# Attention and two feed-forward blocks on one core: instruction order from a list scheduler instead of an order written by hand

## Chip, cores and metric

One Trainium2 chip, 1 core. The metric is the device time of one execution in microseconds (us). The kernel before took 1174.35 us, the median of 3 runs (1172.29 to 1177.39).

## The reference

Three steps over N = 6016 rows, C = 256, all in float32, the weights stored as float64:

```
s    = (k/|k|).T @ (q/|q|) / tau         # 256 x 256, norms over N
a    = softmax(s)                        # over the last axis
x    = v @ a                             # 6016 x 256
xn   = x / sqrt(mean(x*x) + 1e-6) * rms_g
y    = (silu(xn @ w_gate) * (xn @ w_val)) @ w_out       # 256 -> 1536 (twice) -> 256
h    = y @ w_in2
out  = (h - tanh(h)) @ w_out2                           # 256 -> 2048 -> 256
```

## The kernel before

Everything is computed transposed: 128 channels on the partitions, up to 512 rows of N on the free axis. A float32 product is split in a high and a low part of type fp32r (`hi_of` on ScalarE, L138, writes the high part; `lo_of` on VectorE, L144, the rest), and `prod` (L146) issues three matmuls for it: wh·xh, wl·xh, wh·xl. So each operand of TensorE costs one ScalarE and one VectorE instruction. Some small products use full float32 matmuls, which the profile records as two matmuls each.

The work runs in five parts.

1. **Scores** (`attention`, L396): 47 tiles of q and k arrive in 13 chunks; 94 float32 products add up in two PSUM banks, ScalarE squares q and k, VectorE adds the squares. Of the last `BEHIND` = 3 chunks the products for the first bank are issued first, then the norms (`nrm`), then the products for the second bank. `WARM` = 8 float32 products on ones come ahead of the first data.
2. **Softmax, x and its norm** for blocks 0 and 1 (512 and 384 rows): `x_full`, `x_post`.
3. **Gate blocks** (`gate_block`, L1007): block pair 0 with plain products, 12 slices `f` of the hidden width; block 1 runs `SKEW` = 2 slices behind. Beside it the float64 weights are turned to float32 in nine `items` (L255: gv0, gv1, w10, gv2, gv3, w11, gv4, gv5, w12), each of two ScalarE and four VectorE instructions on 128x1024 (`conversion`, L289), and the x of pair 1 (blocks 2 and 3) is made.
4. **Five block pairs of the first feed-forward** with 7 instead of 8 block products (`unit`, L815, twice in each of 6 units, `first_unit`, L863). Each pair also makes the x and the operands of the next pair (`x_operands`, L660, `operands`, L621). The row norm takes a path over DRAM: TensorE sums the squares (`ms`), the row goes out (`row`), comes back narrow (`nar`), VectorE takes the root, it goes out again (`back`) and is broadcast to 128 partitions (`rs`, L765), and VectorE multiplies four x tiles by it (L771). Beside it the weights of the second feed-forward are converted (`second_weights`) and sums of weight blocks are formed (`first_sums`, `second_sums`).
5. **Six block pairs of the second feed-forward** (`second_unit`, L1195), 8 units each.

Products with an output weight (`acc`) are not issued where their operand is made; they wait in a list, `fillers`, and `fill(n)` issues some at fixed places of a `unit`, to occupy TensorE while another engine works on a bank.

The order on each engine is written by hand: main steps as in the code, side work as generators (`Work`) whose next VectorE or ScalarE step is let in by `side(a, d)` at fixed places with fixed counts (`SIDE`, `SIDES`, `EARLY`, `PLAN`). A generator that needs a transfer waits for a number of such places (`yield 4` behind the issue of `rs`). Each engine runs its own queue in order, SyncE (SP) the DMAs' queue.

Of the kernel before, what the change touches and what calls it, by code (L numbers as in the profile page):

```python
# [1 line left out]

# [11 lines left out]
AX = mybir.AxisListType  # L14
# [10 lines left out]
LAST_CHUNKS = [2, 1]  # L25
BEHIND = 3
WARM = 8

EARLY = (((0, 1), (0, 0), (0, 0)), ((0, 1), (0, 0), (0, 0)), ((1, 1), (0, 1), (0, 0)))
SIDES = (((1, 2), (1, 2), (1, 1)), ((1, 2), (1, 2), (1, 1)))  # L30
RSQRT_SEED = float(0x5F3759DF)

REBIAS = 2.0 ** -112


class Work:
# [3 lines left out]


    clock = 0

    def __init__(self, steps):
        self.steps, self.kind, self.ready, self.done = steps, None, None, False

        self.last = dict(A=-1, D=-1, pe=-1)
        self.advance()

    def advance(self):  # L50
        got = next(self.steps, self)
        self.kind = self.ready = None
        if got is self:
            self.done = True
        elif callable(got):
            self.ready = got
        elif isinstance(got, int):
            at = Work.clock + got
            self.ready = lambda: Work.clock >= at
        else:  # L60
            self.kind = got

    def can(self, kind):
        while self.ready and self.ready():
            self.advance()
        return self.kind == kind and self.last[kind] < Work.clock

    def run(self):
        if self.kind in self.last:
            self.last["A" if self.kind == "D" else "D"] = Work.clock  # L70
        self.advance()
# [3 lines left out]
def attn_moe_kernel(  # L75
# [14 lines left out]

# [29 lines left out]
    dram = ctx.enter_context(tc.tile_pool(name="dram", bufs=1, space=bass.MemoryType.DRAM))  # L120

    def bank(tag, name):
        return ps.tile([P, BLK], F32, tag=tag, name=name)
# [5 lines left out]
    def psum(name):  # L129

        turn[0] += 1
        return bank(WORK[(turn[0] - 1) % 4], name)

    def f32(t):
        return t.bitcast(F32)

    def hi_of(dst, src, scale=1.0):
        nc.scalar.activation(out=dst, in_=src, func=AF.Copy, scale=scale)  # L138

    def copy(dst, src):  # L140
        nc.scalar.activation(out=dst, in_=src, func=AF.Copy)  # L141

    def lo_of(dst, src, hi):
        nc.vector.tensor_sub(out=dst, in0=src, in1=f32(hi))  # L144

    def prod(out, w, x, start):  # L146

        (wh, wl), (xh, xl) = w, x
        for i, (a, b) in enumerate(((wh, xh), (wl, xh), (wh, xl))):
            nc.tensor.matmul(  # L150
                out, a, b, start=start and i == 0, stop=i == 2, skip_group_check=True)

    def rsqrt_ops(m, y, t):

        ops = [lambda: nc.vector.tensor_scalar(
            out=y.bitcast(I32), in0=m.bitcast(I32), scalar1=-0.5, scalar2=RSQRT_SEED,
            op0=ALU.mult, op1=ALU.add)]
        for _ in range(3):
            ops += [
                lambda: nc.vector.scalar_tensor_tensor(  # L160
                    out=t, in0=y, scalar=-0.5, in1=m, op0=ALU.mult, op1=ALU.mult),
                lambda: nc.vector.tensor_mul(out=t, in0=t, in1=y),
                lambda: nc.vector.scalar_tensor_tensor(
                    out=y, in0=t, scalar=1.5, in1=y, op0=ALU.add, op1=ALU.mult),
            ]
        return ops

    def add(o, a, b):
        nc.vector.tensor_add(out=o, in0=a, in1=b)  # L169


    works = []

    def side(a=0, d=0):

        Work.clock += 1
        for kind, count in (("D", d), ("A", a)):
            for _ in range(count):
                w = next((w for w in works if w.can(kind)), None)
                if w:  # L180
                    w.run()
        works[:] = [w for w in works if not w.done]


    urgent = []

    def hurry():
        while urgent:
            urgent.pop(0)()

    def between():

        w = next((w for w in works if w.can("pe")), None)
        if w:
            w.run()

    def force(w, until):
        while not until():
            assert not w.done
            w.run()  # L200
            hurry()
# [4 lines left out]
    def narrow_tile(x, b):  # L206
        return wpool.tile([P, NARROW], F32, tag=f"nar{x}", name=f"nar{x}{b}")


    for x in "myt":  # L210
        narrow_tile(x, "")
    tau_t = wpool.tile([P, 1], F32, tag="tau", name="tau_t")
    g_t = wpool.tile([P, KC], F32, tag="g", name="g_t")
# [7 lines left out]
    make_identity(nc, ident)  # L221

    def act_tile(tag, bufs, name, dt=F32R, shape=None):
        return act.tile(shape or [P, BLK], dt, tag=tag, bufs=bufs, name=name)

    def buffer(tag, bufs, dt=F32R):
        return lambda name: act_tile(tag, bufs, name, dt)

    ox, oh, ol = buffer("ox", 5, F32), buffer("oh", 10), buffer("ol", 10)
    ut, uh, ul = buffer("ut", 4, F32), buffer("uh", 4), buffer("ul", 4)
    cs, sq_tile, sq_part = buffer("cs", 3, F32), buffer("sq", 4, F32), buffer("sq", 4)

    V2 = [P, KC, BLK]

# [19 lines left out]
    for i in range(len(w1)):  # L256
        items += [gv[2 * i], gv[2 * i + 1], w1[i]]
    for c in gv:
        c["saved"] = dram.tile([P, W], F32, tag=f"{c['nm']}s", name=f"{c['nm']}s")

    conv_stack = ExitStack()
    conv = conv_stack.enter_context(tc.tile_pool(name="conv", bufs=1))

    def w_load(c):
        c["raw"] = conv.tile([P, W, 2], I32, tag="raw", bufs=2, name=f"{c['nm']}raw")
        part = W // len(c["src"])
        for s, src in enumerate(c["src"]):
            nc.sync.dma_start(
                out=c["raw"][:, s * part:(s + 1) * part, :].rearrange(
                    "p (k n) w -> p k (n w)", k=c["rows"]), in_=src)  # L270

    def w_start(c):

        c["y"] = conv.tile([P, W], F32, tag="y", bufs=2, name=f"{c['nm']}y")
        nc.scalar.activation(
            out=c["y"], in_=c["raw"][:, :, 1].bitcast(F32), func=AF.Copy, scale=REBIAS)

    def shift(y):
        nc.vector.tensor_single_scalar(out=y, in_=y, scalar=3, op=ALU.logical_shift_left)

    def sign(y, high):
        nc.vector.scalar_tensor_tensor(
            out=y, in0=high, scalar=-0x80000000, in1=y, op0=ALU.bitwise_and, op1=ALU.bitwise_or)

    def bits(y, word):
        nc.vector.scalar_tensor_tensor(
            out=y, in0=word, scalar=29, in1=y, op0=ALU.logical_shift_right, op1=ALU.bitwise_or)

    def conversion():  # L289

        yield "D"
        w_start(items[0])
        for i, c in enumerate(items):
            y = c["y"].bitcast(I32)
            yield "D"
            shift(y)
            yield "D"
            sign(y, c["raw"][:, :, 1])  # L300
            yield "D"
            bits(y, c["raw"][:, :, 0])
            if "saved" in c:
                nc.sync.dma_start(out=c["saved"], in_=c["y"])
            c["h"], c["l"] = (
                wpool.tile([P, W], F32R, tag=f"{c['nm']}{x}", name=f"{c['nm']}{x}") for x in "hl")
            yield "A"
            hi_of(c["h"], c["y"])
            if i + 2 < len(items):
                w_load(items[i + 2])  # L310
            if i + 1 < len(items):
                yield "A"
                w_start(items[i + 1])
            yield "D"
            lo_of(c["l"], c["y"], c["h"])
            c["ready"] = True

    converter = Work(conversion())

    def part(c, at, n=P):  # L320
        return c["h"][:, at:at + n], c["l"][:, at:at + n]

    def first_weight(x, kk, f):
        return part(gv[f // 2], x * 2 * C + kk * 2 * P + f % 2 * P)

    def out1_weight(f, m):
        rows = W // C
        need(w1[f // rows])
        return part(w1[f // rows], f % rows * C + m * P)
# [8 lines left out]

    late = []

    def block_sums(y):

# [209 lines left out]
    xn = {}  # L554
# [758 lines left out]
```

## Time and profile before

| | |
|---|---|
| median of 3 runs | 1174.35 us |
| span of the profiled execution, first to last instruction | 1178.0 us |
| PE (matmul) busy | 1139.4 us, 97% |
| PEld (weight load) busy | 932.8 us, 79% |
| DVE (VectorE) busy | 821.6 us, 70% |
| ACT (ScalarE) busy | 687.6 us, 58% |
| mean granted TensorE clock | 0.988 of 2.4 GHz |
| DMA moved | 76.72 MB |

The profiled execution's own time is known as its span alone; it lies 3.65 us above the median and 0.6 us above the slowest run. A matmul's record reaches from its start to the modelled arrival of its last column, so records of successive matmuls overlap, and a short gap between two starts does not show as idle time of PE.

### The profile page before, as it was taken

To read this page: it belongs to the slowest core of one execution; us is meant where nothing else is said; L and a number is where in the kernel's file an instruction comes from. 1 tells how busy PE (TensorE), PEld (TensorE's weight loads), DVE (VectorE), ACT (ScalarE), POOL (GpSimd) and SP (SyncE) were. 2 spreads that over 40 slices of the span, in tenths; PEclk is the share of its full clock that TensorE was granted. 3 is DMA by queue.
4 is the path that set the end of the run, shared out by engine and by line. 5 is a ranking of instruction groups with operands and counts; after the bars stand their busy time and mean duration, and the time that the engine had idled before them with its cause. 6 is when DMAs were issued, how large, how long until landed. Compare 5 with 4: busy or idle time off the path is not lost.

```text
span 1178.0 us, 13953 instructions
## 1 busy us (share of the span) xinstructions
PE 1139.4 (97%) x4980; PEld 932.8 (79%) x4980; DVE 821.6 (70%) x1374; ACT 687.6 (58%) x1199; POOL 0.7 (0%) x6
## 2 busy tenths in 40 slices
PE   9889899999999999999999999999999999999998
PEld 8668687777778787777878889888788788788787
DVE  5877676667677767676776687776776776776665
ACT  6444547546646754664565576655655656656655
POOL 0000000000000000000000000000000000000000
PEclk9989998999999999999999999999999999999999
DMA  9535222121321312112041220100100100100000
GB/s 361 215 107 195 77 68 69 53 72 34 110 72 37 119 52 73 55 70 55 25 125 50 67 78 10 43 26 1 63 10 1 63 10 1 63 1 1 36 1 36
DMA packets 41193, 76.72 MB, mean 65 GB/s; under 512 B 6810, under 2 KB 11674, under 8 KB 41124
## 3 DMA queue, kind: packets, MB, share of 16 engines
q1 hardware_dynamic: 40836, 74.79, 19.0%
q10 hardware_dynamic: 288, 1.05, 0.2%
q8 instruction: 39, 0.64, 0.2%
q14 instruction: 30, 0.25, 0.1%
HBM read 54.02 MB, written 21.80 MB: 64 GB/s over the span
## 4 chain that ended last, share of the span: by engine, by line
PE 77%; DVE 10%; DMA 6%; ACT 4%; issue 2%; SPq 0%; DVEq 0%; ACTq 0%
PE acc L150 32%; PE Yh L150 8%; PE Xh L150 5%; PE Yv L150 5%; PE Yg L150 5%; PE Xg L150 3%; PE Xv L150 3%; PE Th L150 3%; PE Zh L150 3%; DMA k<-k_in 2%; PE x L150 2%; DMA rs<-back 2%; PE Tg L150 2%; PE Tv L150 2%; PE Zv L150 1%
## 5 line engine op out<-in xcount | busy, mean ns | idle before, releaser
L138 ACT ACTIVATE hc<-wc 128x512 fp32r<-128x512 f32 (+1 forms) x192 | 113.9, 617 | 82.6 <-DVE wc L1203 81.4
L144 DVE TENSOR_TENSOR lc<-wc,hc 128x512 fp32r<-128x512 f32 (+1 forms) x192 | 126.5, 675 | 33.2 <-ACT hc L138 33.2
L138 ACT ACTIVATE uc<-t 128x512 fp32r<-128x512 f32 x120 | 72.3, 628 | 111.1 <-DVE t L846 111.1
L144 DVE TENSOR_TENSOR ulc<-t,uc 128x512 fp32r<-128x512 f32 x120 | 79.7, 685 | 3.5 <-ACT uc L138 0.6
L169 DVE TENSOR_TENSOR Zv<-Yv,m5v 128x512 f32<-128x512 f32 x30 | 21.0, 700 | 83.2 <-ACT x_1g L689 42.0
L169 DVE TENSOR_TENSOR Zh<-Yh,m5h 128x512 f32<-128x512 f32 (+1 forms) x48 | 33.0, 688 | 51.1 <-PE Yh L150 47.6
L1203 DVE TENSOR_TENSOR wc<-Yh,wc 128x512 f32<-128x512 f32 (+1 forms) x48 | 32.7, 681 | 28.2 <-ACT wc L1200 28.1
L1200 ACT ACTIVATE wc<-Yh 128x512 f32<-128x512 f32 (+1 forms) x48 | 28.3, 590 | 35.7 <-PE Yh L150 35.7
L1200 ACT ACTIVATE wc<-Xh 128x512 f32<-128x512 f32 (+1 forms) x48 | 28.4, 591 | 32.8 <-PE Xh L150 32.8
L169 DVE TENSOR_TENSOR Zg<-Yg,m5g 128x512 f32<-128x512 f32 x30 | 21.0, 699 | 36.3 <-PE Yg L150 28.4
L1200 ACT ACTIVATE wc<-s 128x512 f32<-128x512 f32 (+1 forms) x48 | 30.0, 624 | 25.9 <-DVE s L169 25.3
L169 DVE TENSOR_TENSOR s<-Yh,m5h 128x512 f32<-128x512 f32 (+1 forms) x48 | 32.6, 679 | 17.8 <-PE Yh L150 16.8
L430 PE MATMUL S<-q,k 128*128 128x256 f32 x188 | 43.4, 395 | 0.9 <-DMA k<-k_in 0.9
L430 PEld LDWEIGHTS S<-q,k 128*128 128x128 f32 x188 | 37.2, 199 | 6.5 <-DMA k<-k_in 1.1
L1203 DVE TENSOR_TENSOR wc<-s,wc 128x512 f32<-128x512 f32 (+1 forms) x48 | 32.7, 682 | 8.8 <-ACT wc L1200 8.8
L849 ACT ACTIVATE t<-Zg 128x512 f32<-128x512 f32 x30 | 18.0, 599 | 31.3 <-PE Zg L150 31.2
L150 PE MATMUL Yh<-T2h,l2s 128*128 128x512 f32 (+1 forms) x96 | 29.9, 392 | 4.5 <-ACT Yh L141 4.4
L1203 DVE TENSOR_TENSOR wc<-Xh,wc 128x512 f32<-128x512 f32 (+1 forms) x48 | 32.6, 680 | 1.2 <-ACT wc L1200 0.6
L435 DVE TENSOR_TENSOR acc<-acc,sq 128x1024 f32<-128x1024 f32 (+1 forms) x24 | 24.1, 1023 | 13.5 <-ACT sq L460 12.8
L1203 DVE TENSOR_TENSOR wc<-Zh,wc 128x512 f32<-128x512 f32 (+1 forms) x48 | 32.3, 672 | 0.0
L141 ACT ACTIVATE r<-acc 128x512 f32<-128x512 f32 (+2 forms) x48 | 27.2, 580 | 7.2 <-PE acc L150 6.9
L150 PE MATMUL acc<-uc,w11h 128*128 128x512 f32 x80 | 31.4, 393 | 0.0
(918 smaller groups left out, 3502.1 us busy)
## 6 DMA issues: line engine op xcount, KB each, us to landing
q<-q_in SPq DMA_DIRECT2D x11, 512.0 KB, 6.9
vraw<-vT_in SPq DMA_DIRECT2D x11, 512.0 KB, 3.7
y<-r SPq DMA_DIRECT2D x22, 256.0 KB, 2.0
y<-y SPq DMA_DIRECT2D x20, 256.0 KB, 2.7
outT<-r SPq DMA_DIRECT2D x20, 256.0 KB, 2.0
k<-k_in SPq DMA_DIRECT2D x9, 512.0 KB, 10.3
raw<-w_in_in SPq DMA_DIRECT2D x8, 512.0 KB, 3.9
l<-y SPq DMA_DIRECT2D x16, 256.0 KB, 3.3
```

The lines of the kernel that those rows point to most:

```text
L138: nc.scalar.activation(out=dst, in_=src, func=AF.Copy, scale=scale)
L141: nc.scalar.activation(out=dst, in_=src, func=AF.Copy)
L144: nc.vector.tensor_sub(out=dst, in0=src, in1=f32(hi))
L150: nc.tensor.matmul(out, a, b, start=start and i == 0, stop=i == 2, skip_group_check=True)
L169: nc.vector.tensor_add(out=o, in0=a, in1=b)
L430: nc.tensor.matmul(S[m][:, :C], kt[:, j, m * P:(m + 1) * P], qt[:, j, :], start=(i == 0 and j == 0), stop=(i == NCH - 1 and j == chunks[i] ...
L435: nc.vector.tensor_add(out=out, in0=a, in1=b)
L849: nc.scalar.activation(out=o, in_=a, func=AF.Silu)
L1200: nc.scalar.activation(out=t[c][:, :n], in_=src, func=AF.Tanh)
L1203: nc.vector.tensor_sub(out=t[c][:, :n], in0=src, in1=t[c][:, :n])
```

## The change

The functions build a graph of operations first; nothing is issued while they run. Each operation has an engine, a cost in nanoseconds, the operations it depends on and, on TensorE, a `key`. `schedule` plans the start of each in six rounds and keeps the order of the round whose planned end is earliest; then the instructions are issued in that order. `Buf`, `Part` and `Slot` find the dependences, a tile's reuse included. `LAG0/1/2` set how far behind the main products an `acc` product ranks.

Beside that: `WARM` 8 to 11, `BEHIND` 3 to 5 (the adding up of squares keeps 3, now `FOLDED`), the order of the first three items is gv0, w10, gv1, the sums of w_in2 are formed at its own conversion, and the x of block 2 (first half of the thread of pair 1) stands behind the first norm of block 0, ahead of the norm of block 1, in banks a0 and a1; the loads of blocks 2 and 3 of v stand behind those of blocks 0 and 1. The second half follows at slices 2 and 4 of block 1.

```
-PLAN = {
-    ("s", 4): 1, ("s", 5): 1, ("s", 6): 1, ("s", 7): 1, ("s", 12): 2, ("c", 1): 3, ("c", 2): 1,
-    ("c", 3): 2, ("f", 0): 1, ("f", 1): 0,
-}
-BEHIND = 3
-WARM = 8
+LATENCY = {
+    ("PE", "PE"): 0, ("PE", "ACT"): 262, ("PE", "DVE"): 262,
+    ("ACT", "PE"): 152, ("DVE", "PE"): 140, ("DVE", "ACT"): 120, ("ACT", "DVE"): 132,
+    ("ACT", "ACT"): 130, ("DVE", "DVE"): 116,
...
+COLD = 7000.0
+PATIENT, HOLD, TOLERANCE = ("ACT", "DVE"), 600.0, 60.0
+DMA_SETUP, DMA_RATE, DMA_TAIL, DMA_ISSUE = 1000, 385.0, 900, 450
...
+        def rank(o):
+            return (o.key if o.eng == "PE" else o.idx if o.late is None else o.late, o.idx)
...
+            t, e = best
+            while known[e] and known[e][0][0] <= t:
+                o = ops[heappop(known[e])[1]]
+                heappush(avail[e], (*rank(o), o))
+            o = heappop(avail[e])[2]
+            if e in PATIENT and o.late is not None:
+                o = self.patient(o, t, known[e], avail[e], ops, lag)
...
+            if e == "SP":
+                free[e] = t + DMA_ISSUE
+                wire = max(t + DMA_SETUP, wire) + o.size / DMA_RATE
+                o.end = wire + DMA_TAIL
+            else:
+                o.end = free[e] = t + o.cost * (2 if e == "PE" and t < COLD else 1)
...
+def act_cost(n, psum=False):
+    return n / 1.2 + (60 if psum else 94)
+
+def dve_cost(n, inputs=2):
+    return 65 + n / (0.96 * (3 - inputs))
+
+ROUNDS = 6
+FOLDED, BEHIND = 3, 5
+WARM = 11
+LAG0, LAG1, LAG2 = 4100.0, 9500.0, 4800.0
...
-        items += [gv[2 * i], gv[2 * i + 1], w1[i]]
+        items += [gv[2 * i], gv[2 * i + 1], w1[i]] if i else [gv[0], w1[0], gv[1]]
...
+        return g.op("PE", 3 * (n / 2.4 + 13.7), emit, [wh, wl, xh, xl], [out], key=key)
...
+            prod(o, self.weight(f, m), u, n, i == 1, key=g.main + self.lag)
...
+    p0["spread"]()
+    for c in range(KC):
+        p0["rest"](c)
+        p1["gain"](c)
+    x_next = {}
+    x_banks = ["a0", "a1"]
+    thread = x_thread(
+        1, lambda name, c: bank(x_banks.pop(0), name) if x_banks else psum(name), x_next)
+    next(thread)
+    p1["rs"]()
+    p1["spread"]()
...
+    X_AT = {(1, 2): 1, (1, 4): 1}
...
+    for o in g.schedule(ROUNDS):
+        o.emit()
```

In a plan PE takes, of the operations whose inputs have come, the one with the lowest key; ACT, DVE and SP take the one with the smallest `late`, the latest start that the round before allowed. `patient` lets ACT and DVE wait up to 600 ns for a more urgent one.

## Rows read from the trace of the kernel before

**Rows 1.** The page: busy time, share of the span and instructions of each engine.
```profile
PE 1139.4 (97%) x4980; PEld 932.8 (79%) x4980; DVE 821.6 (70%) x1374; ACT 687.6 (58%) x1199; POOL 0.7 (0%) x6
```

**Rows 2.** Five stretches: length, then PE, PEld, DVE, ACT, POOL busy (instructions), PEclk, DMA.
```profile
5.72:46.23 40.51, 40.14 (x175) 34.65 (x175) 31.21 (x35) 26.02 (x28) 0.00 (x0) 1.00 0.99 384
46.23:66.73 20.50, 17.08 (x78) 11.70 (x78) 12.65 (x46) 10.18 (x19) 0.00 (x0) 0.92 0.31 105
66.73:172.76 106.03, 99.17 (x435) 80.99 (x435) 78.10 (x134) 51.31 (x87) 0.00 (x0) 0.95 0.30 100
172.76:689.10 516.34, 500.51 (x2147) 402.93 (x2147) 359.00 (x627) 298.70 (x531) 0.00 (x0) 0.99 0.22 68
689.10:1174.03 484.93, 478.59 (x2132) 399.02 (x2131) 340.12 (x533) 299.19 (x536) 0.00 (x0) 1.00 0.07 24
```

**Rows 3.** Timeline of PE: start, length, engine, line, operation.
```profile
5.72 8.62 PE L430 MATMUL S<-q,k 128*128 128x256 f32 x28 [0.85 <-DMA k<-k_in]
...
34.69 11.17 PE L430 MATMUL S<-q,k 128*128 128x256 f32 x51
...
93.56 0.39 PE L150 MATMUL acc<-u,w10h 128*128 128x512 f32 x1
...
93.79 0.40 PE L150 MATMUL acc<-u,w10l 128*128 128x512 f32 x1
...
687.51 0.36 PE L150 MATMUL Xh<-B11h,l21h 128*128 128x448 f32 x1
687.71 0.37 PE L150 MATMUL Xh<-B11h,l21l 128*128 128x448 f32 x1
```

**Rows 4.** Timeline of the softmax and of the first norm.
```profile
47.32 0.17 DVE L500 TENSOR_SCALAR n__377<-nrm 128x8 f32<-128x8 f32 x1 [0.81 <-PE nrm L490]
...
53.92 6.04 PE L560 MATMUL x<-vraw,a 128*128 128x512 f32 x10 [2.69 <-DVE sm L534]
...
59.14 0.60 ACT L572 ACTIVATE sq<-x 128x512 f32<-128x512 f32 x1 [3.95 <-PE x L560]
...
66.73 0.50 PE L150 MATMUL g<-xh,gv0h 128*128 128x512 f32 x1 [0.28 <-ACT xh L138]
```

**Rows 5.** Waits of PE: who waited for whom, total us, times, longest.
```profile
PE Yv L150 <- DVE c L169: 7.5, 5, 1.9
...
PE ms L717 <- ACT sh L138: 2.5, 1, 2.5
...
PE acc L150 <- DVE w10l L144: 1.8, 1, 1.8
```

**Rows 6.** Timeline of two of the five waits of Yv, with what stood ahead.
```profile
211.10 0.42 DVE L347 TENSOR_TENSOR s<-s 128x256 f32<-128x256 f32 x1 [2.24 <-DMA s<-gv5s]
...
212.18 0.50 PE L150 MATMUL Yv<-T4h,gv1h 128*128 128x512 f32 x1 [1.33 <-DVE c L169]
...
451.45 0.69 DVE L771 TENSOR_TENSOR x_0g<-x_0g,rs 128x512 f32<-128x512 f32 x1 [2.55 <-DMA rs<-back]
452.06 0.69 DVE L169 TENSOR_TENSOR c<-Yv,m5v 128x512 f32<-128x512 f32 x1
...
452.81 0.50 PE L150 MATMUL Yv<-T4h,gv3h 128*128 128x512 f32 x1 [1.91 <-DVE c L169]
```

**Rows 7.** DMA issues: operation, count, size, median us to landing.
```profile
vraw<-vT_in SPq DMA_DIRECT2D x11, 512.0 KB, 3.7
...
y<-y SPq DMA_DIRECT2D x20, 256.0 KB, 2.7
...
raw<-w_in_in SPq DMA_DIRECT2D x8, 512.0 KB, 3.9
...
rs<-back SPq DMA_DIRECT2D x10, 256.0 KB, 3.9
```

**Rows 8.** The chain that ended last: two of its transfers of `back`.
```profile
159.01 1.54 DMA back<-naryp
...
444.61 2.96 DMA back<-naryp
```

More of the change, by code (lines that the diff above doesn't have):

```diff
@@ L168, in add @@
[L168 to L195, printed above, removed]
@@ L289, in conversion @@
[L289 to L316, printed above, removed]
@@ new lines, in attention, with load @@
+        S = [bank(ACC[0][m], f"S{m}") for m in range(KC)]
+        nrm = bank("b0", "nrm")
+        raw = {}
+        def load(i):
+            t0, n = chunks[i]
+            raw[i] = []
+            for s, (src, nm) in enumerate(((qr, "q"), (kr, "k"))):
+                pool, *tags = lent[i % len(lent)]
+                r = new(pool, tags[s], f"{nm}{i}", [P, CH, C])
+                size = n * C * P * 4
+                from_ = src[:, t0:t0 + n, :]
+                if s and i < 2:
+                    g.op("SP", 0, lambda r=r, n=n, a=from_: nc.scalar.dma_start(
+                        out=r.t[:, :n, :], in_=a), (), [r], size=size)
+                else:
+                    dma(r[:, :n, :], from_, size, (), [r])
+                raw[i].append(r)
@@ new lines, in attention @@
+        load_v(0)
+        load_v(1, "vh")
+        load_v(2, "vl")
+        load_v(3, "wraw")
+        dma(tau_t, tau.to_broadcast([P, 1]), 512, (), [tau_t])
+        dma(g_t, rms_g, 1024, (), [g_t])
+        NN = 2 * 2 * KC
+        rest = [(i, j) for i in range(NCH - BEHIND, NCH) for j in range(chunks[i][1])]
+        for i, j in rest:
+            score(i, j, 0)
+        for s in range(2):
+            for m in range(KC):
+                c0 = 2 * (KC * s + m)
+                matmul(nrm[:, c0:c0 + 2],
+                       sums(s, lambda t, s=s, m=m: t[:, s, 0, m * P:(m + 1) * P]),
+                       ones[:, :2], 2 * 24, True, True)
@@ L608, in high @@
[L608 to L621 removed]
+            tt("mul", x, x, T["y"][:, :n], n)
@@ L657, in operands, with x_thread @@
-        out["late"] = True
-        yield from split(("B22", b22), ("T4", t2))
-    def x_operands(p, take, last, out):
+        yield
+        split("B21", b21)
+        split("T3", b12)
+        split("B22", b22)
+        split("T4", t2)
+    def x_thread(p, take, out):
         B = []
-        row = dram.tile([2, BLK], F32, tag="row", name=f"row{p}")
-        back = dram.tile([2, BLK], F32, tag="back", name=f"back{p}")
+        row, back = (new_dram(f"{x}{p}", [2, BLK]) for x in ("row", "back"))
@@ L751, in x_operands @@
[L751 to L761 removed]
+                matmul(o, mean, x, BLK, i == 0, i == 1, full=False)
@@ L1063, in finish_late @@
-    def finish_late(w, x):
-        while "late" not in x:
-            w.run()
-            hurry()
-        urgent.append(lambda: finish(w))
-    finish(x_work)
+            gate_block(1, f - SKEW)
+            for _ in range(X_AT.get((1, f - SKEW), 0)):
+                next(thread)
+    for _ in thread:
+        pass
     for tag in "YZ":
-        nc.tensor.matmul(bank(tag, f"{tag}first"), mean, x_next["B11"][0], start=True, stop=True)
+        matmul(bank(tag, f"{tag}first"), mean, x_next["B11"][0], BLK, True, True, full=False)
```

1528 lines of the change are left out of this document (765 added, 763 removed).

## The prediction

> **What bounds the kernel now.** I read the page's first part, then stretches of the trace, then the timeline of single places. The page has PE busy 97% of the span [rows 1], 38.6 us idle. That is too small a number for what can be won, since the records overlap. Successive matmuls of 512 columns start 0.23 us apart though each record lasts 0.39, those of 448 columns 0.20 apart (687.51, 687.71); so 64 columns are worth 0.027 us, and 384 columns 0.173 [rows 3]. I use 0.227 for 512, the two-digit starts bearing 0.22 to 0.24: 2132 records of the last stretch, about 350 of them narrow, make 350 x 0.200 + 1782 x 0.227 = 474.5 of its 484.9 us, and a larger pitch than 0.232 would not fit [rows 2]. A score record, half a float32 product, takes 11.17/51 = 0.219 us; I use 0.215, since the last record's tail is in the 11.17. A 512-wide float32 record is then 0.43 [rows 3].
>
> With these, each stretch splits into matmul work and loss [rows 2]:
>
> - 5.72 to 46.23 (scores): 175 x 0.215 = 37.7 of 40.5; loss 2.8. The first 28 take 8.62 us, 0.308 each, against 0.219 later [rows 3]: 2.5 us of it is the slow start.
> - 46.23 to 66.73 (softmax, x, norm): scores 14 x 0.215, x 8 x 0.43 + 8 x 0.325, and some 48 short records at about 0.11 (two columns or a spread), 14.4 in all; loss 6.1.
> - 66.73 to 172.76 (gates): 288 gate records, half 512, half 384 wide, 57.6; about 120 acc records, half of each, 24.0; x 16 x 0.43 = 6.9; others 2: 90.5. Loss 15.5.
> - 172.76 to 689.10 (five pairs): 2147 x 0.227 = 487.4; loss 28.9.
> - 689.10 to 1174.03 (six pairs): loss 10.4.
>
> That is 63.7 us in which TensorE neither multiplies at full speed nor is at an end of the kernel; the 5.72 ahead and 4.0 behind are a first transfer and a last copy and store. The clock column says which part of the loss is half-speed time: (1 - 0.92) x 20.5 + 0.05 x 106 + 0.01 x 516 = 12.1 us [rows 2], in the stretches that also hold the longest waits. DVE, the next engine, is busy 74% in the gates, 70% in both rows of pairs [rows 2]: no other engine is full. So TensorE is the bound, and what the change can reach is these 63.7 us.
>
> **The change part by part.**
>
> *Matmul work* stays: the same products, splits and conversions are issued. `WARM` adds 3 products, 6 records of about 0.21 as later scores of twice the columns show, 1.3 us; the 0.85 us of waiting for k hides most of it [rows 3], 0.2 to 0.4 can stick out. If PE then reaches full speed sooner, up to 2.5 us come back; if not, nothing. I take half: 1.5 of 2.8 left.
>
> *Softmax and first norm.* From the first VectorE step on the norms (47.32) to x (53.92) are 6.6 us, of which PE waited 2.69 at the end [rows 4]. `BEHIND` 5 leaves 15 products for the second bank behind the norms, 30 x 0.215 = 6.5 us, against 7 products, 3.0 us, before: the 6.6 us are covered. The softmax of the second bank alone, an estimated third of the 6.6, lies beside the four x products with the first half of `a` (1.7 + 1.3 us). From the first square (59.14) to the first gate (66.73) are 7.6 us [rows 4]; beside them can now lie the last x of block 1 (1.3), the ms and spread records (4.0) and, new, x of block 2, 8 x 0.43 = 3.4: 8.7 us. Left of 6.1: 1.0; the bounds are 0 and, if a late square keeps the cover from fitting, 3.5, what the waits left there before. The 3.4 us of x are moved, not new. With them go two SP loads of v, 512 KB each, ahead of the gates, where DMA is 31% busy [rows 2]; square, gain and the sum over the channels come on ACT and DVE between the norms, 4 x 0.6 and 2 x 0.6 us, where these engines are busy 50 and 62%. What follows them in DVE's queue is the norm of block 1, needed two slices later.
>
> *Gates.* The wait of ms for `sh`, 2.5 us [rows 5], goes: its operand is then made some 60 us ahead. The wait for w10l, 1.8 [rows 5], goes if VectorE converts w10 in time; gates now start about 3 us earlier (1.3 + 5.1 less lost, 3.4 of x more done), so with less half-speed time it must be done by about 77 instead of 84.5. DVE stood idle for 20.5 - 12.65 = 7.8 us in the stretch ahead and 28 in the gates [rows 2]: two items of 4.4 us fit, without much to spare. I leave 4.0 of 15.5; 0 and 10 are the bounds, 10 being all that is not half speed.
>
> *The five pairs.* The named wait is Yv for `c`, 7.5 us in five [rows 5]. Its place shows the mechanism: VectorE stands 2.55 us at the product with `rs`, whose transfer has not landed, and `c`, which PE needs, is queued behind it; PE waits 1.91 us [rows 6]. The other case is the same with a load of a saved weight (2.24, then 1.33). So 0.6 to 0.9 us of such a halt are absorbed. The planner prices a transfer at 1.0 + size/385 + 0.9: 2.58 us for `rs`, and the trace has 3.9; 3.26 for v and raw weights, and the trace has 3.7 and 3.9; 2.58 for y, trace 2.7 [rows 7]. Since VectorE has idle time, the plan sets the product right behind the planned landing, and the real one is 1.3 us later. `back`, priced at 1.91, took 1.54 to 2.96 [rows 8], 0.3 over by the middle of that range. With nothing absorbed, five times 1.6 us stay: 8.0. The loads that land 0.4 to 0.6 late fall under what is absorbed and I count none. The rest of the 28.9 goes: the planner's VectorE price, 0.598 us for 512 columns, is the trace's (0.61 between 451.45 and 452.06 [rows 6]), so where no transfer is in the chain the plan should hold. Bounds: 3, and 20, when all 35 late landings of this part cost half a us more.
>
> The Trainium skill, "DMA: Bandwidth & Descriptors", section Specifications, says that pieces under 512 B are read, modified and written back; `back` is written in pieces of 16 B, and the plan knows its bytes alone. By that every `back` would be like the slowest, 2.96 us, 1.05 over instead of 0.3, and the sum 3.8 us longer, 1131; the trace has one at 1.54 too, so I go by the middle.
>
> *The six pairs.* Their loss sits at pair ends, where acc products and the next operands meet; here loads land as planned. Left: 2.0 of 10.4, bounds 0 and 6.
>
> Sum: 1.5 + 1.0 + 4.0 + 8.0 + 2.0 = 16.5 left, 63.7 - 16.5 = 47.2 less, 1178.0 - 47.2 = 1130.8 by the profiled execution. That lies 3.65 above the median; the runs should show about **1127**.
>
> **The rivals.**
>
> *The plan holds nearly everywhere.* For it: prices that match to 2%; against: the transfers. 5 us left, 1119 in the span, 1116 in the runs. The floor, nothing left, is 1111.
>
> *Half comes back.* VectorE becomes the bound up to the first acc products: w10 and gv1 are late again, which leaves the gates their 10 us, halts on transfers leave the pairs 20, and 5 stay elsewhere. 35 us left: 1146.
>
> *The change doesn't do what it says*: the plan's order is, where it matters, the hand's order, or new waits weigh up the old. Within 0.5%, 1174. Against it: the waits named above have their operand moved.
>
> *Slower.* Place: queues of VectorE and ScalarE in the pairs. By hand, a transfer's consumer stood several places behind its issue; in the plan it stands at its planned landing, with PE-feeding steps behind. About 85 landings have such a consumer (10 rs, 5 m, 8 v, 16 raw weights, 6 + 16 saved ones, 24 y). If each held PE 1.3 us, as the 1.91 and 1.33 of [rows 6] less some cover, that is 110 us: 1178 - 64 + 110 = 1224, 1220 in the runs. It decides from 64/85 = 0.75 us per landing. Against it: [rows 7] has most of them late by 0.1 to 0.6 only, and that is absorbed.
>
> **How the numbers follow.** Forecast 1127 with its own range 1116 to 1140 (16.5 left, 5 to 30): 0.58. Nearly everywhere: 0.15. Half: 0.13. No change: 0.05. Slower: 0.09. About 0.5% is what a measurement of this kernel can tell from no change, 1168.5 to 1180.2. Faster: 0.58 + 0.15 + 0.13 = 0.86; same 0.05; slower 0.09. For 8 in 10 the range takes the forecast, most of the first rival and the half: 1112 to 1150.
>
> **What would show it.** In the profile after: the stretch from the last score to the first gate without a wait of PE over 0.7 us; no wait of ms for `sh` or of acc for w10; score records under 0.25 us each from the start or not; the pairs 98% matmul work, with any wait of Yv standing behind VectorE at `rs`; fewer half-speed stretches (a clock of 0.995 or more). Wrong would be: waits of PE on VectorE of over 0.5 us in each unit (the slower rival), or a loss of over 8 us in the gates with VectorE busy over 90% there.

## The result and the profile after

The changed kernel takes 1147.21 us, the median of 4 runs (1146.56 to 1148.4), against 1174.78 of the kernel before in the same session: ratio 0.9773 [0.9752, 0.9795], 27.6 us less. The forecast was 1127, a gain of 47. Direction and range held; the size was too large by 20 us.

The profiled execution of after has a span of 1145.3 us, 32.7 below the one of before. It took 1147.1 us by itself, so 1.8 us lie around a span, and it stands at its median; the one of before, 1178.0 + 1.8, stood 5 us above its own. So of the 20.2 us that the forecast missed, 14.5 are in the trace (a span of 1130.8 was forecast), and 5.5 are in the step from span to median: I took 3.65 off as if the new profile would be a high sample too, and added nothing for what lies around it.

The page's first part for after:

```profile
PE 1125.6 (98%) x4986; PEld 927.1 (81%) x4986; DVE 817.5 (71%) x1376; ACT 694.0 (61%) x1199; POOL 0.7 (0%) x6
```

The stretches that answer to [rows 2], cut at the same places of the work (first score, first norm, first gate, first pair); the last cut is at the first product of the second feed-forward, 653.85. Columns as there:

```profile
5.56:44.99 39.43, 38.30 (x175) 32.82 (x174) 32.70 (x39) 27.81 (x30) 0.00 (x0) 1.00 1.01 394
44.99:71.21 26.22, 21.38 (x87) 13.65 (x87) 19.72 (x57) 16.12 (x28) 0.00 (x0) 0.87 0.66 224
71.21:163.36 92.15, 91.57 (x440) 79.06 (x440) 75.96 (x137) 49.71 (x87) 0.00 (x0) 1.00 0.28 92
163.36:653.85 490.49, 482.19 (x2082) 388.03 (x2081) 339.68 (x600) 288.41 (x510) 0.00 (x0) 1.00 0.22 67
653.85:1141.36 487.51, 487.51 (x2185) 409.20 (x2183) 348.91 (x543) 309.72 (x546) 0.00 (x0) 1.00 0.07 24
```

The reader is to see three things. The gates and the last part are full: PE is busy 91.57 of 92.15 and 487.51 of 487.51 us. The five pairs still have 8.3 us of plain gaps of PE. In the kernel before, that last product starts at 677.69; cut there, and not at 689.10 as in [rows 2], the five pairs take 504.92 us with 15.8 us of gaps, so they have become 14.4 us shorter. And the stretch from the first norm to the first gate, which was to become clean, is the one with the half-speed time: a clock of 0.87 over 26 us, though the matmuls of x of block 2 are in it now, 3.4 us.

Loss is counted below as in the prediction: from a record's start to the next one's, less the price of its width. Record by record, from the start of the span, this makes 66.6 us for the kernel before (the prediction's sums by stretch made 63.7, without the first products):

| us lost in the span | 0–40 | 40–80 | 80–180 | 180–700 | 700–end | sum | of it half speed |
|---|---|---|---|---|---|---|---|
| before | 3.8 | 9.8 | 17.0 | 28.1 | 7.9 | 66.6 | 13.1 |
| after | 1.1 | 10.0 | 3.6 | 17.3 | 0.7 | 32.6 | 5.0 |

So what was won lies in the gates (13.4 us), the five pairs (10.8), the six pairs (7.2) and the start (2.7), and nothing was won between 40 and 80 us. 8.1 us of it is less time at half speed. The "half speed" is the lower of TensorE's two levels, 1.2 GHz, granted for 6.8 us from 52.7 on and for 3.4 us from 349.7 on in after; both stretches begin in or behind a long wait of PE shown below.

PE's longest waits in after, beside the first ones for data, and the one wait of DVE that stands behind most of them (who waited for whom, total us, times, longest):

```profile
PE Yv L407 <- DVE c L388: 5.2, 4, 2.4
PE x L415 <- DVE a L773: 3.0, 1, 3.0
...
PE rq_ps L415 <- DVE r__448 L741: 1.0, 1, 1.0
```

```profile
DVE x_0g L388 <- DMA rs<-back: 16.3, 7, 4.9
```

The waits of ms for `sh` and of acc for `w10l` [rows 5] are gone, as forecast. The wait of Yv for `c` is not: 5.2 us against 7.5. One place of it, of PE's, DVE's and ACT's rows (start, length, engine, line, operation):

```profile
345.55 0.69 DVE L388 TENSOR_TENSOR x_0g<-x_0g,rs 128x512 f32<-128x512 f32 x1 [1.70 <-DMA rs<-back]
...
346.28 0.63 ACT L373 ACTIVATE B11h<-x_0g 128x512 fp32r<-128x512 f32 x1 [4.44 <-DVE x_0g L388]
...
347.60 0.69 DVE L388 TENSOR_TENSOR x_0g<-x_0g,rs 128x512 f32<-128x512 f32 x1 [0.76 <-DMA rs<-back]
348.21 0.68 DVE L388 TENSOR_TENSOR c<-Yv,m5v 128x512 f32<-128x512 f32 x1
...
348.95 0.50 PE L407 MATMUL Yv<-T4h,gv4h 128*128 128x512 f32 x1 [2.43 <-DVE c L388]
...
350.30 0.69 ACT L373 ACTIVATE y<-raw 128x512 f32<-128x512 f32 x1 [2.79 <-DMA raw<-w_in_in]
```

DVE stands twice at a product with `rs` that has not landed, and `c`, which PE needs, is queued behind the second: the mechanism of [rows 6], with ACT held by the same halt for 4.44 us and, 4 us on, by a raw weight for 2.79. The plan thought these transfers had landed. Their landing in after (count, KB each, median us from issue to landing):

```profile
vraw<-vT_in SPq DMA_DIRECT2D x11, 512.0 KB, 4.2
...
raw<-w_in_in SPq DMA_DIRECT2D x8, 512.0 KB, 4.4
...
l<-y SPq DMA_DIRECT2D x16, 256.0 KB, 4.2
rs<-back SPq DMA_DIRECT2D x10, 256.0 KB, 4.1
```

The planner prices 512 KB at 3.26 and 256 KB at 2.58 us when nothing is ahead on its wire. A saved block `l` that is issued 0.45 us behind a raw weight, as 15 of the 16 are in the planned order, comes to 3.49 by its formula. These medians rest on few transfers, since the trace has the landing of some only: four of the 16 raw weights landed at 3.78 to 4.39; seven of 16 `l` at 4.03 to 4.53; four of ten `rs` at 3.46 to 4.50; the two v of the pairs that start from an idle wire at 3.58 and 3.63, while the 4.2 is drawn up by a v among the scores (7.28) and one behind two other loads (4.77). So raw weights and saved blocks land 0.5 to 1.1 us late, `rs` 0.9 to 1.9 and v 0.3 to 0.6, where the prediction had 0.4 to 0.6 for the loads and 1.3 for `rs`. The raw weights of `w_in` landed at 3.53 to 3.99 before and at 4.25 to 4.39 in after, three known landings each.

### The profile page after: what moved, and what is told of

It reads as the page before. It is cut to its first block, busy times and chain, and to the rows that moved or that the text cites. A ratio compares the mean times of both kernels' runs of the same rounds, so it can differ in the third digit from the quotient of the medians.

```text
span 1145.3 us, 14185 instructions
## 1 busy us (share of the span) xinstructions
PE 1125.6 (98%) x4986; PEld 927.1 (81%) x4986; DVE 817.5 (71%) x1376; ACT 694.0 (61%) x1199; POOL 0.7 (0%) x6
## 4 chain that ended last, share of the span: by engine, by line
PE 76%; DVE 11%; DMA 8%; ACT 3%; issue 2%; SPq 0%; DVEq 0%; ACTq 0%
PE acc L407 33%; PE Yh L407 8%; PE Xh L407 6%; PE Yv L407 4%; PE Yg L407 4%; PE Zh L407 3%; PE Th L407 3%; PE Xg L407 3%; PE Xv L407 2%; DMA rs<-back 2%; PE g L407 2%; PE v L407 2%; DVE tc L388 2%; DVE ulc L392 1%; DMA raw<-w_out_in 1%
## 5 line engine op out<-in xcount | busy, mean ns | idle before, releaser
L392 DVE TENSOR_TENSOR ulc<-wc,uc 128x512 fp32r<-128x512 f32 (+1 forms) x192 | 130.2, 679 | 83.8 <-ACT uc L373 81.4
L373 ACT ACTIVATE uc<-wc 128x512 fp32r<-128x512 f32 (+1 forms) x192 | 119.5, 623 | 103.2 <-PE acc L407 91.4
L373 ACT ACTIVATE uc<-tc 128x512 fp32r<-128x512 f32 x120 | 73.4, 628 | 81.4 <-DVE tc L388 81.0
L392 DVE TENSOR_TENSOR ulc<-tc,uc 128x512 fp32r<-128x512 f32 x120 | 78.5, 683 | 2.7 <-ACT uc L373 2.4
L388 DVE TENSOR_TENSOR wc<-Yh,wc 128x512 f32<-128x512 f32 (+1 forms) x48 | 32.6, 678 | 10.3 <-ACT wc L373 10.3
L373 ACT ACTIVATE wc<-Yh 128x512 f32<-128x512 f32 (+1 forms) x48 | 28.2, 586 | 15.2 <-PE Yh L407 14.5
L373 ACT ACTIVATE r<-acc 128x512 f32<-128x512 f32 (+2 forms) x48 | 27.3, 587 | 15.8 <-PE acc L407 11.3
L373 ACT ACTIVATE m5h<-Th 128x512 f32<-128x512 f32 (+1 forms) x48 | 28.2, 588 | 11.5 <-PE Th L407 11.5
L373 ACT ACTIVATE tc<-Xg 128x512 f32<-128x512 f32 x30 | 17.9, 598 | 27.9 <-PE Xg L407 27.7
L373 ACT ACTIVATE Yh<-Xh 128x512 f32<-128x512 f32 (+1 forms) x48 | 27.6, 575 | 11.7 <-PE Xh L407 10.3
L373 ACT ACTIVATE tc<-Zg 128x512 f32<-128x512 f32 x30 | 17.9, 597 | 25.7 <-PE Zg L407 20.2
L388 DVE TENSOR_TENSOR tc<-Yg,m5g 128x512 f32<-128x512 f32 x30 | 20.7, 690 | 16.0 <-PE Yg L407 15.6
```

Of the source, the lines that this page charges most:

```text
L373: nc.scalar.activation(out=ap(out), in_=ap(in_), func=func, **{x: ap(a) for x, a in kw.items()})
L388: return dve(lambda: f(out=ap(out), in0=ap(a), in1=ap(b)), n, 2, [a, b], [out])
L392: lambda: nc.vector.tensor_sub(out=ap(out), in0=ap(in_), in1=f32(ap(hi))), n, 2,
```

## The experiments

Two disputes stood: what the late landings cost (the prediction counts `rs` alone; its slower rival counts all 85), and what the stretch from the norms to the gates lacks. All ratios are to the kernel before, with their 95% intervals. Its median was 1174.78, 1177.54, 1176.94 and 1176.39 us in the four sessions, so a difference of some 3 us between the medians of two sessions can come from the session.

**Only `rs` priced later.** The planner's price of `rs` gets 2.0 us more, of `back` 0.5.

```
-                o.end = wire + DMA_TAIL
+                o.end = wire + DMA_TAIL + o.more    # rs: 2000, back: 500, else 0
```

> The changed kernel, but the plan prices the broadcast of the row norms (rs) 2.0 us and its way out (back) 0.5 us higher, near what the trace of the changed kernel shows for them (rs 3.9 to 4.7 us against a price of 2.58); nothing else differs but the order that follows. Theory 1 (late landings: VectorE stands at the product with rs, 16.3 us in 7 waits, and what PE needs is queued behind): the waits of VectorE on rs fall below 6 us, the two long waits of Yv at 244 and 346 us go, and the time falls by 4 to 8 us from 1147, to 1139 to 1143. Rival (these waits are absorbed; the loss of the five pairs comes from many small late handovers): the waits on rs fall as well, but the time stays within 1.5 us of 1147.

1141.92 us, ratio 0.9706 [0.9678, 0.9735]: 5.3 less than after, as expected. DVE's waits on `rs` fall from 16.3 to

```profile
DVE x_0g L388 <- DMA rs<-back: 0.2, 1, 0.2
```

and Yv's on `c` from 5.2 to 1.2. The loss of the five pairs falls from 18.7 to 14.8: so `rs` costs some 3.9 us there, by the mechanism that the prediction had for its 8.0; the other 1.4 lie ahead of the pairs, where the new plan differs too. The place at 345 shows what is late next: PE stood there 2.13 us behind ACT instead, which waited for a raw weight:

```profile
347.92 0.66 ACT L373 ACTIVATE y<-raw 128x512 f32<-128x512 f32 x1 [3.91 <-DMA raw<-w_in_in]
348.49 1.65 ACT L373 ACTIVATE uc<-tc 128x512 fp32r<-128x512 f32 x3
350.05 0.57 ACT L373 ACTIVATE Yg<-Xg 128x512 f32<-128x512 f32 x1
...
350.68 0.50 PE L407 MATMUL Yg<-T2h,sh 128*128 128x512 f32 x1 [2.13 <-ACT Yg L373]
```

**Every transfer priced later.** As above, and `DMA_TAIL` 900 to 1700, so that 512 KB are priced at 4.06 us and 256 KB at 3.38.

> As e1, and besides every transfer is priced 0.8 us later (tail 1.7 instead of 0.9 us), near what the trace shows for raw weights, saved weights and v (3.7 to 4.8 us against 3.26). Theory 1: a further 3 to 6 us less than e1, 1134 to 1139, with ScalarE's waits on raw weights (12.5 us in 9) mostly gone. Rival (loads that land 0.4 to 1 us late are absorbed, as the prediction had it): within 1.5 us of e1. Third possibility: the later price delays q and k in the plan and costs the scores 1 to 3 us.

1133.05 us, ratio 0.9628 [0.9601, 0.9656]: another 8.9 less, more than the 3 to 6 expected. This is the term that the prediction set to nothing; the loss between 180 and 700 us falls from 14.9 to 4.4. The known landings now lie near their prices: raw weights at 4.17 and 4.50 and v at 3.73 and 3.80 against 4.06, a saved block at 4.15 against 4.29. In the pairs PE waits for nothing over 0.7 us any more; its list begins with the two waits of the softmax:

```profile
PE x L415 <- DVE a L773: 2.7, 1, 2.7
PE rq_ps L415 <- DVE r__449 L741: 2.3, 1, 2.3
...
PE Yg L407 <- ACT Yg L373: 0.7, 1, 0.7
PE g L407 <- ACT xh L373: 0.6, 1, 0.6
```

**Every transfer priced earlier.** The changed kernel with `DMA_TAIL` 900 to 100: the opposite sign, and the slower rival's ground.

> The changed kernel with every transfer priced 0.8 us earlier (tail 0.1 instead of 0.9 us): the dose the other way. Theory 1: if a landing that the plan has too early halts an engine with PE's work behind it, each tenth counts; e2 won 9 us beyond e1 by 0.8 us on the others, so 6 to 16 us more than the changed kernel, 1153 to 1163. Rival (a halt costs only beyond a threshold that most loads are past already, or the gain of e2 came from another order by chance): within 3 us of 1147.

1177.27 us (10 runs), ratio 1.0009 [0.9991, 1.0026]. A price that is 0.8 us lower in one constant takes the whole gain away, 30 us by the medians and 28 by the ratios, nearly twice the most that was expected. The list of PE's waits has Yv on top again, now behind another step of the same queue:

```profile
PE Yv L407 <- DVE Zv L388: 11.9, 6, 2.6
```

Four of the six waits are of 2.3 to 2.6 us and have VectorE at `rs` ahead of them; one place of the timeline:

```profile
365.10 0.69 DVE L388 TENSOR_TENSOR x_0g<-x_0g,rs 128x512 f32<-128x512 f32 x1 [4.73 <-DMA rs<-back]
...
367.52 0.69 DVE L388 TENSOR_TENSOR Zv<-Yv,m5v 128x512 f32<-128x512 f32 x1
...
368.26 0.50 PE L407 MATMUL Yv<-T3h,gv4h 128*128 128x512 f32 x1 [2.50 <-DVE Zv L388]
```

Most of PE's other waits of over 0.7 us in the pairs follow, within 6 us, a halt of ScalarE at a raw or saved weight.

**Priced still later.** In the kernel with both prices and held conversions (told below), `DMA_TAIL` 1700 to 2500.

> As e7 (rs and back priced higher, conversions held), with every transfer priced at another 0.8 us later: 2.5 in place of 1.7 for the tail. Theory 1 (only landings that come later than planned cost, and at 1.7 all of them are covered): nothing more to win; a longer price only lengthens the planner's own chains, 0 to +4 us against e7, so 1131 to 1135, ratio 0.961 to 0.965. Rival (the tail of the landing times is still uncovered, since the slowest of them lie 2 us over their price): another 2 to 5 us, 1126 to 1129.

1131.88 us, ratio 0.9629 [0.9589, 0.967], against 1130.88 at 1700. Nothing more comes, and next to nothing goes. By `DMA_TAIL`, then: 100 is +30 us against 900; 1700, with `rs` and `back` priced higher, -14; 2500 no better. Late prices are nearly free, early ones are not.

**The hand order with `rs` later.** The kernel before, with one number changed: the consumer of `rs` waits for two more places.

```
             nc.sync.dma_start(out=rs[t], in_=back[t:t + 1, :].to_broadcast([P, BLK]))
-        yield 4
+        yield 6
```

> The kernel before, in its hand-written order, with one edit: the multiplication by the row norms is let in 6 instead of 4 places behind the issue of rs. Theory 1 (in both kernels the loss of the five pairs comes from VectorE standing at a transfer with PE's work behind it): VectorE's waits on rs fall from 11.9 us to below 4, four of the five waits of Yv go, 5 to 10 us less than before. Rival (what is late moves on to the operands that follow): the time stays within 2 us of before, with new waits of B11 or Xg at the ends of pairs.

1172.92 us (10 runs), ratio 0.9966 [0.9953, 0.998], 4.0 less, between the two expectations. The waits of DVE on `rs` and of Yv on `c` are gone from the lists, and a third of their 7.5 us came back elsewhere: Yg's waits for ACT's Yg grew from 1.7 to

```profile
PE Yg L150 <- ACT Yg L141: 4.3, 3, 1.7
```

So the longest wait of the kernel before was worth at most 4.0 of the some 28 us of the change; it doesn't carry the gain. (At most, since the one profile of this kernel also lacks the slow start, some 2 us, and whether its other executions do isn't known.)

**The conversions held back until the squares are added.** In the changed kernel DVE converts gv0 and w10 between 26.2 and 31.2 us and then, but for one more conversion step at 35.7, adds squares without a pause until 45.8. Here the first conversions depend on the last folds.

```
+        for o in folds:                       # the last adds of the squares
+            g.ops[-1].preds.setdefault(o, False)
```

> The changed kernel, but no weight is converted before the squares of q and k are added up: the first instruction of each conversion waits for the last of these sums. In the changed kernel VectorE converts gv0 and w10 for 6 us between 26 and 37 us and then adds without a pause until 46.5, and x starts at 53.9. Theory 2 (the way from the sums over the norms to x sets the start of x, and VectorE's load sets the sums): the sums end 3 to 5 us earlier, x starts at 49 to 51.5, PE's waits for r, a and acc (4.6 us together) shrink below 2, and the time falls by 2 to 6 us unless gv0 or w10 then come late for the gates, which would show as waits of the first g or acc. Rival (the landing of the last q and k sets the sums): x starts at 53 or later and the time stays within 1.5 us.

1148.36 us, ratio 0.9758 [0.9719, 0.9796]: no change in the time. PE around the norms, first in after, then here:

```profile
45.01 0.61 PE L415 MATMUL nrm<-ones,acc 128*128 128x2 f32 x4 [0.60 <-DVE acc L388]
45.47 1.11 PE L415 MATMUL S<-q,k 128*128 128x256 f32 x4
46.42 0.50 PE L415 MATMUL nrm<-ones,acc 128*128 128x2 f32 x4
46.78 2.40 PE L415 MATMUL S<-q,k 128*128 128x256 f32 x10
50.20 0.68 PE L415 MATMUL rq_ps<-ident,r__448 128*128 128x128 f32 x4 [1.01 <-DVE r__448 L741]
53.91 2.93 PE L415 MATMUL x<-vraw,a 128*128 128x512 f32 x3 [3.02 <-DVE a L773]
```

```profile
43.87 0.61 PE L416 MATMUL nrm<-ones,acc 128*128 128x2 f32 x4
44.33 1.11 PE L416 MATMUL S<-q,k 128*128 128x256 f32 x4
45.28 0.50 PE L416 MATMUL nrm<-ones,acc 128*128 128x2 f32 x4
45.64 3.27 PE L416 MATMUL S<-q,k 128*128 128x256 f32 x14
49.05 0.68 PE L416 MATMUL rq_ps<-ident,r__427 128*128 128x128 f32 x4
52.42 4.13 PE L416 MATMUL x<-vraw,a 128*128 128x512 f32 x10 [2.69 <-DVE a L777]
```

The local effect is there, but small: the first norm comes 1.1 us earlier, not 3 to 5, and x at 52.42, 1.5 earlier, between the two expectations. VectorE, with nothing to convert, stood still instead until ScalarE's squares came, and then added without a pause until 44.7:

```profile
30.44 6.36 DVE L389 TENSOR_TENSOR acc<-acc,sq 128x1024 f32<-128x1024 f32 x5 [5.55 <-ACT sq L374]
```

So the conversions had mostly filled a pause, and the adding behind it is most of what sets the sums. The loss between 40 and 80 us still falls from 10.0 to 5.6, with none of it at half speed. But the loss between 80 and 180 rises from 3.6 to 5.4 (acc waits 1.6 us for `u`) and between 180 and 700 from 17.3 to 19.9: the plan shifted. That other late landings then reached PE is likely, by the next run, but was not followed wait by wait.

**Both: prices and held conversions.**

> e2 and e3 together: later prices for all transfers, and no conversion before the sums of squares. Theory 2 in its remaining form (e3 won 4 to 5 us ahead of the first gate, and lost them to transfers that the plan had too early): with right prices they stay won, 1126 to 1131 against 1133 of e2. Rival (VectorE's load up to the first acc products is the limit, what is held comes late there): 1132 or more, with a wait for w10.

1130.88 us, ratio 0.9616 [0.9591, 0.9641]: 2.2 less than prices alone. The single runs don't overlap (1130.62 to 1132.53 against 1132.56 to 1133.43), but the intervals of the two ratios, from two sessions, do; so that the gain of the held conversions stays once the landings are priced right is likely and no more.

**`BEHIND` 3 in place of 5**, on top of both.

> As e7, with BEHIND 3 in place of 5: 7 products of the second bank are keyed behind the norms, not 15. Theory 1 (TensorE takes whatever is ready, so what is keyed behind the norms is spent before them all the same when the sums come late): within 1.5 us of e7, 1129.5 to 1132.5, and as many score records behind the first norm record. Rival (the prediction's step: 15 products cover the softmax): 8 products are 3.4 us less cover, 1133 to 1135.

1130.17 us, ratio 0.9615 [0.9568, 0.9661]: the same as with 5. 14 score records stand behind the first norm record, as in after:

```profile
44.04 0.50 PE L416 MATMUL nrm<-ones,acc 128*128 128x2 f32 x4
44.41 0.68 PE L416 MATMUL S<-q,k 128*128 128x256 f32 x2
44.92 0.50 PE L416 MATMUL nrm<-ones,acc 128*128 128x2 f32 x4
45.28 2.84 PE L416 MATMUL S<-q,k 128*128 128x256 f32 x12
```

So `BEHIND` gives no cover by its size. The planner lets PE take whatever is ready; while the sums are awaited it takes the products that were to cover the softmax. The other planned kernels say the same: with 5, 10 to 18 score records stand behind the first norm record, with 3, 10 to 14; the 30 that the prediction counted on stand there in none.

**x of block 2 back among the gates.** The changed kernel, with the thread of pair 1 started in the gates as before.

```
-    next(thread)
-    X_AT = {(1, 2): 1, (1, 4): 1}
+    X_AT = {(1, 1): 1, (1, 3): 1, (1, 5): 1}
```

> The changed kernel without its second part: x of block 2 is not beside the first norms but among the gates (after slice 1 of block 1, the rest after slices 3 and 5), in the common banks; the order is planned in the same way. Theory 3 (x of block 2 covers the chain from the first square to the first gate): PE waits 2 to 3.4 us more between the last x of block 1 and the first gate, the time rises by 1 to 4 us. Rival (the planner fills that place with other work, or x of block 2 only moves): within 1 us of the changed kernel.

1151.28 us, ratio 0.9784 [0.9756, 0.9813]: 4.1 more than after by the medians, and the single runs don't overlap (1150.67 to 1152.3 against 1146.56 to 1148.4); but the intervals of the two ratios, from two sessions, do. The loss between 40 and 80 us is 13.8 instead of 10.0, 6.6 of it at half speed. That is the part which belongs to x of block 2; elsewhere this plan loses 1.4 more before 40, 1.4 more between 80 and 180 and 2.6 less between 180 and 700.

**The planner alone.** The changed kernel with all the small edits taken back: `WARM` 8, `BEHIND` 3, the old order of the conversions, x of block 2 among the gates.

> The planner without the other edits: WARM 8, BEHIND 3, items in the old order, x of block 2 among the gates. From e4 the place of x of block 2 is worth 4 us; WARM is expected to give 2 (no slow start in the changed kernel, 2.5 us of it before), BEHIND and the items 0 to 2. So 1152 to 1156, and the planner's order alone makes some 20 of the 27 us. Rival (the small edits make most of the gain): 1160 or more.

1148.2 us, ratio 0.9766 [0.9739, 0.9794], the same as the full change and better than the 1152 to 1156 expected. Together the small edits seem worth nothing. But the trace says otherwise: 0 to 80 us lose 17.2 instead of 11.1, and 180 to 700 lose 13.8 instead of 17.3. In the pairs of this plan fewer halts reach PE (Yv waits 0.7 us for `c` instead of 5.2); nothing in the edits aims at that, so it is put down to chance here.

**The same with right prices.** The small edits taken back from the kernel with every transfer priced later.

> As e2 (rs, back and every transfer priced later), but with the small edits of the change taken back: WARM 8, BEHIND 3, the old order of the conversions, x of block 2 among the gates. Theory 1 (with right prices the losses ahead of the pairs are all that is left, so the small edits show): 3 to 7 us slower than e2, 1136 to 1140, from 3.7 of slow start and some 3 of half clock. Rival (they cancel, as in e6 against the full change): within 1.5 us of e2, 1131.5 to 1134.5.

1137.64 us (1136.97 to 1138.68), ratio 0.9679 [0.964, 0.9719], against 1133.05 (1132.56 to 1133.43) with them: 4.6 us. With 4 us lost in the pairs of both, the small edits show; the profiled spans differ by 6.1, of which 3.3 are the slow start and 5.4 the stretch from 40 to 80, less 1.3 of `WARM` not issued and 1.3 of smaller losses later. The two were not run in one session; by their ratios the difference is 6 us.

**`WARM` 8 alone**, a single run.

> The changed kernel with WARM 8 in place of 11, one look for the first 20 us of the trace. Theory 1 (the three extra products close the gap of TensorE between its first products and the first score, so that the clock comes up earlier): the first scores come at 0.42 us a record again up to about 10 us, and some 3.7 us are lost there. Rival (the start is quicker because q and k arrive earlier in the planned order): the first scores at 0.22 us each as in the changed kernel.

1141.55 us, one run. Its first scores come at full pace; those of the planner alone, with the same gap of 0.9 us in front of them, at half. Two stretches of each (columns as in [rows 2]), first the planner alone, then this one:

```profile
5.70:8.00 2.30, 2.25 (x5) 1.85 (x6) 0.00 (x0) 1.85 (x2) 0.00 (x0) 1.00 1.04 424
8.00:10.50 2.50, 2.50 (x7) 2.01 (x6) 1.13 (x1) 2.22 (x3) 0.00 (x0) 1.00 1.03 418
```

```profile
5.70:8.00 2.30, 2.20 (x10) 1.97 (x11) 0.00 (x0) 1.91 (x2) 0.00 (x0) 1.00 1.03 422
8.00:10.50 2.50, 2.50 (x14) 2.19 (x13) 1.26 (x2) 2.35 (x3) 0.00 (x0) 1.00 1.04 419
```

Neither expectation is borne out: the old gap does not always bring the slow start, and earlier data are not the reason, since the first score starts at 5.80. The five profiles with the gap of `WARM` 8 (before, the hand order with `rs` later, the planner alone, the same with right prices, this one) have the slow start three times; the nine with `WARM` 11 never. The 1.00 in the clock column of the planner alone is no reading: the trace's records of the granted clock begin at 10.61 us there (10.44 in before, 10.66 in the kernel with the edits taken back and right prices), and the column counts time without a record as full speed. In the eleven profiles without the slow start the records begin at 4.5 to 6.6 us, at the latest 0.6 us behind the first score. Scores 0.43 us apart ahead of 10.6, and 0.22 behind it, are those of the two levels, 1.2 and 2.4 GHz. So the slow start is a clock that was raised only some 5 us behind the first score; in the two profiles with the gap but without the slow start it was up at 4.46 and 4.92, the gap beginning at 4.74 and 4.86. That this kernel is also 5.7 us below after is not the slow start but the pairs, 13.3 us lost instead of 17.3, and the gates. So one small edit ahead of the pairs moves what the pairs lose by 4 us: a difference of this size between two plans is no proof by itself, and needs the waits beside it.

The loss by stretch, counted as above, of the kernels on which the argument rests:

| us lost | 0–40 | 40–80 | 80–180 | 180–700 | 700–end | sum |
|---|---|---|---|---|---|---|
| after | 1.1 | 10.0 | 3.6 | 17.3 | 0.7 | 32.6 |
| `rs` priced later | 1.6 | 8.9 | 1.4 | 14.9 | 0.5 | 27.2 |
| every transfer later | 0.6 | 10.2 | 2.2 | 4.4 | 0.6 | 18.1 |
| and held, `BEHIND` 3 | 0.9 | 7.9 | 2.8 | 3.4 | 0.3 | 15.2 |
| every transfer earlier | 1.4 | 10.2 | 9.5 | 38.0 | 3.0 | 62.1 |
| planner alone | 3.9 | 13.4 | 3.1 | 13.8 | 0.5 | 34.5 |
| planner alone, right prices | 4.0 | 15.6 | 1.2 | 4.2 | 0.6 | 25.5 |

## Why the prediction was right in direction and too high in size

| stretch | loss forecast | loss in after |
|---|---|---|
| scores | 1.5 | 2.0 |
| softmax, x, norm | 1.0 | 8.5 |
| gates | 4.0 | 2.3 |
| five pairs | 8.0 | 18.7 |
| six pairs | 2.0 | 1.3 |
| sum | 16.5 | 32.8 |

1147 with 32.8 us of loss is, as a number, the rival "Half comes back" (1146, 35 left), which the range took in. Its 20 us for halts on transfers in the pairs are near the 18.7 found; its 10 in the gates, with VectorE as the bound, are not there (2.3), and the 8.5 between the norms and the gates stand in neither it nor the forecast. That its sum fits is in part luck. Of the signs named ahead, two failed: PE waits 3.02 and 1.01 us between the last score and the first gate, and the pairs are 96% matmul work (18.7 of 490.49 us lost), not 98.

*That TensorE's lost time is what the change can reach* held: no other engine is full in any stretch of after (VectorE, the next, is busy 83% at most, in the scores), and repairing prices and conversions brings the kernel to 1130.2 with 15.2 us of loss, near the 16.5 that the forecast gave the change itself.

*The five pairs* is the step that failed most. "The loads that land 0.4 to 0.6 late fall under what is absorbed and I count none": pricing them right gained 8.9 us. Two errors made it. The halt that [rows 6] shows being absorbed in part was in the hand order, where several places lie between a landing and its consumer; in the plan the two halts at 345 (1.70 and 0.76 us) cost PE 2.43, so nothing of them was absorbed. And the size of the lateness was read in the old order, from medians of [rows 7] behind which two or three known landings stand (`vraw` two, the raw weights and `rs` three each), and which also left out the 16 loads `l<-y`: known landings of 2.15, 3.27 and 4.41 in before, where they were issued ahead of their raw weights, and 4.03 to 4.53 in after, where they are issued behind them. The Trainium skill, "DMA: Bandwidth & Descriptors", section "Latency and other measured facts", gives the access to device memory (HBM) 0.2 us on average and 2 us at high load. The 2.15 had no transfer issued in the 6.5 us ahead of it, so the trace agrees that neighbours make a landing later; how much of that is access and how much waiting behind the other bytes no run here shows. The named part, `rs`, was over-priced: 8.0 against some 3.9 in the pairs and 5.3 in all. The slower rival had the right mechanism, but not its size: it put 0.75 us or more on each of 85 landings, and after loses 18.7 in its pairs; the run with earlier prices is its world, and there the gain is gone to the last us.

*Softmax and norms*, 1.0 forecast and 8.5 found: "`BEHIND` 5 leaves 15 products for the second bank behind the norms, 30 x 0.215 = 6.5 us". After the first norm record 14 records were left, not 30, some 3.0 us; then PE waited 1.01 and 3.02 us, and of the 6.8 us at half speed 5.6 lie behind the start of x, 2.8 lost. I had read a rank as a place. In a planner that never lets PE idle, a product keyed behind another is only issued behind it if that other one is ready; with the sums late, the cover was spent first. Of the sums' lateness, the weights that DVE converts between 26 and 31 us make 1.1 us, by the run that holds these back; that `BEHIND` itself is without effect is shown by the run with 3. What is left there in the best kernel is 7.9 us between 40 and 80, 2.7 of them the wait for `a`; no run here removes it. That a cover of 6.5 us would be enough if it were held back is not shown either.

*x of block 2* was right in kind: moved back, 3.8 us more are lost between 40 and 80, and the time rises by 4.1.

*Gates and six pairs* were right, and better than forecast: both waits named went. That the plan's VectorE and ScalarE prices hold where no transfer stands in the chain fits this, but no run tests it.

*The slow start*: the 1.5 of 2.8 were half a guess; it went altogether in after. The profiles tie it to a clock that rose only some 5 us behind the first score, in three of the five kernels with a gap of PE in front of it and in none of the others; they show no more.

*"The changed order is no better by itself"* (the rival of no change) is excluded by the planner alone: 0.9766.

*What stays open*: why one plan, by luck, loses 4 us less in the pairs than another (after against `WARM` 8 alone) was not followed wait by wait; and why the clock was up in time in two of the five profiles with the gap and not in the other three.

## What to carry to other kernels

A list scheduler sets a consumer right at the time it thinks its operand lands, in a queue that then stops everything behind it: price a transfer at the upper end of what the trace shows under load, since 0.8 us less on a price that was already early cost 30 us here, and 0.8 us more on one that met the landings cost 1 us or nothing. Read landings again after the order has changed, for every kind of load, not for the one that stands in the list of waits. And test a small edit only after such errors are out: with early prices the edits of this change measured as nothing, with later ones as 4.6 us.

## What the runs showed of the hardware that I had not expected

- The clock column can hide a slow start: in the planner alone 12 score records take the 4.8 us from 5.70 to 10.50 in which 24 fit in the run with `WARM` 8, and the column reads 1.00 in both, since the trace of the first has no record of the clock ahead of 10.61 us. The distance between starts, 0.43 against 0.22 us, shows it.
- The runs of the kernel before lie between 1170.31 and 1180.34 us in one session and follow the mean granted clock (0.997 at the fastest, 0.989 at the slowest). A single profile can stand 5 us from its median, which is a fifth of this result.
- A load's landing depends on what is issued just ahead of it: a saved block `l<-y`, 256 KB, landed 2.15 us behind its issue with nothing issued in the 6.5 us ahead, 3.27 and 4.41 us with a v of 512 KB issued 1.33 and 0.60 us ahead, and 4.03 to 4.53 us (seven known landings) when a raw weight of 512 KB was issued 0.4 us ahead.
